# One core: idle TensorE products in the attention stage, and a new order of its scans, transposes and loads

## The chip, the cores and the metric

The kernel runs on one core of a Trainium2 chip. The metric is the device time of one execution in microseconds; three runs are shown and their median counts. One further execution was profiled: it has a time of its own and a span, the stretch from the first to the last instruction that the profiler recorded.

## The reference

Three parts run one after the other, all in float32.

```python
# attention with a decaying state: batch 4, 8 heads, 768 positions, head size 32, state size 16
for each chunk of 32 positions:
    L = causal(exp(cum_i - cum_j))            # products of the decays a between j and i
    y = (C B^T * L) x + (C state) * exp(cum)
    state = exp(sum log a) * state + B^T (x * decay to the chunk's end)
x = y as [3072 tokens, 256]
h = max(max(x @ w1, x @ w2), x @ w3);  x = h @ w_out          # 256 -> 768 -> 256
out = (sigmoid(x @ w_gate) * (x @ w_val)) @ w_out2            # 256 -> 1536 -> 256
```

## The kernel before, in words

**Attention steps.** The kernel uses chunks of 96 positions, eight of them, and 32 sequences (batch times head). A step (`attention(k, ahead)`, L321) is one chunk and four sequences, so there are 64 steps, eight per chunk. Each step has these parts, parted by `yield`, so that a pipe (`Pipe`, L56) can advance many steps by one part per tick:

- TensorE multiplies B and C into a bank `s` (L332 for the first 16 steps, in float32, where ACT first makes a masked copy of C, L327; L335 later, in bfloat16, from `bi` and `cs`);
- POOL writes the state's part of `mt` (L340) and VectorE multiplies `s` with the decays into `mt` (L347; from step 24 on every other step goes over ACT and POOL, L343 to L345);
- `prepare(k)` (L377) loads and prepares what later steps need;
- TensorE multiplies `mt` with x into the bank `y` (L356). For the first 12 steps (START) each step does its own, later the fourth of four steps does them for all four;
- at every fourth step ACT rounds `y` to `xt_hi` (L366), VectorE subtracts for `xt_lo` (L368), and four VectorE transposes carry the new state into the next chunk's `xs` (L372).

The decays of two steps are one tile `dec` of 388 KB, loaded with a broadcast (L269) into one of four buffers; VectorE turns it into products of decays with a pair of scans (`decay`, L283, L291). A buffer comes free when the two steps that use it are done, so a load of decay n+4 stands behind step 2n+1.

**Parts of B and C.** From chunk 2 on, `split_bc(c)` (L294) loads `bc` (L297) and splits it into three bfloat16 parts, one per tick: ACT casts (L303), POOL subtracts (L312), and SyncE issues 12 DMAs that spread the parts into `bi` and `cs` (L308). Step 16 is the first that needs them.

**Weights.** The first feed-forward layer has six pieces m, each in two halves, `a00`, `a01` to `a50`, `a51`, of two loads of 256 KB each (L150). The table BEHIND (L53) says behind which decay load how many halves are issued. `decode` (L153) unpacks each: ACT three times (L165, L170, L174), VectorE once (L178), POOL once (L183), then ACT rounds (L211) and POOL subtracts (L213). `weights_tick` (L216) puts the next loaded half into the pipe.

**The order.** The stage ahead of the feed-forward part is the loop at L530: 12 steps enter the pipe, one per tick, and `s` runs two ticks more ahead of VectorE's product (LEAD). Nine more ticks follow, each with one decode (L536). Then the first layer runs over six tiles of 512 tokens (L556), six pieces m each, in four slots per piece: three groups of six products into `u` (L406 to L408 by way of `layer`, L497) and the group for the output `o` of the piece before (`down`, L412). At every slot's end the table UNTIL says how many attention steps must have been put into the pipe; in the first tile these are steps 12 to 23. Each group is evicted by `most` (L481): ACT copies (L484), VectorE takes the maximum twice (L486, L488), ACT rounds (L477), and POOL or VectorE subtracts (L479).

Every engine, and SyncE's queue of DMAs, takes its instructions in one fixed order. The compiler makes that order ahead of time; work that it holds to be ready sooner may be issued ahead of its place in the code. `tc.issue_after(i)` holds what is traced inside it behind instruction `i` in the order of that instruction's engine, without a wait for its end. The second feed-forward part (L597 on) is not touched.

Of the kernel before, what the change touches and what calls it, by code (L numbers as in the profile page):

```python
# [8 lines left out]
F32 = mybir.dt.float32  # L9
F32R = mybir.dt.float32r  # L10
BF16 = mybir.dt.bfloat16
F16 = mybir.dt.float16
I32 = mybir.dt.int32
U32 = mybir.dt.uint32
AF = mybir.ActivationFunctionType
ALU = mybir.AluOpType
# [3 lines left out]
CH = 96  # L20
# [22 lines left out]
FIRST = 2 * NG  # L43
MASKED = 8
SHARED = 24
LEAD = 2
MTS = 8
DECS = 4
# [1 line left out]
SLOT = {1: 0, 2: 1, 6: 3, 5: 4, 7: 6, 3: 2, 4: 5}  # L50
WEIGHT = {1: 0, 2: 2, 3: 1, 4: 3, 5: 4, 6: 5, 7: 6}

BEHIND = {4: 1, 5: 1, 6: 2, 7: 2, 8: 2, 9: 1, 10: 1, 11: 1, 12: 1}  # L53


class Pipe:  # L56
# [15 lines left out]
def scan_attention_then_ffn(ctx: ExitStack, tc: tile.TileContext, xh, ah, bch, pick, bn, w1, w2, w3,  # L72
# [56 lines left out]
    def piece1(m, part):  # L129
# [3 lines left out]
                 [up1[2][:, :, cols], dn1[:, m, :].rearrange("p (d f) -> p d f", d=2)]][part]  # L133
        return wp1, wt1.setdefault(m, []), loads, f"a{m}{part}"

    todo = [(piece1, m, part) for m in range(M1) for part in range(2)]
    loaded = []

# [5 lines left out]
    def load_weights():  # L144

        f, m, part = todo.pop(0)
        wpool, blocks, loads, name = f(m, part)
        raw = wpool.tile([128, 2 * len(loads), 128, 2], I32, tag=name, name=f"raw_{name}")
        for k, s in enumerate(loads):
            sp.dma_start(out=raw[:, 2 * k:2 * k + 2].rearrange("p b n t -> p b (n t)"), in_=s)  # L150
        loaded.append((raw, wpool, blocks, name))

    def decode(raw, wpool, blocks, name):  # L153
        nb = raw.shape[1]
        second = name[0] != "a"

        def behind(k):
            return tc.issue_after(evict[k].ins) if second else ExitStack()

        f1 = raw[..., 1]  # L160
        r = stp.tile([128, DEC // 128, 128], I32, tag="r", bufs=3, name=f"r_{name}")[:, 0:nb]
        sg = sgs[len(blocks_done) % len(sgs)][:, 0:nb]
        blocks_done.append(name)
        with behind(0):
            act.activation(out=sg.bitcast(F16).rearrange("p b (n t) -> p b n t", t=2)[..., 1], in_=f1.bitcast(F32),  # L165
                           func=AF.Identity, scale=2.0 ** -112)
        if second:
            yield
        with behind(0):
            act.mul(f1.bitcast(F32), f1.bitcast(F32), 2.0 ** -112)  # L170
        if second:
            yield
        with behind(0):
            act.mul(r, raw[..., 0].bitcast(U32), 2.0 ** -29)  # L174
        yield
        t = stp.tile([128, DEC // 128, 128], I32, tag="t", bufs=2, name=f"t_{name}")[:, 0:nb]
        with behind(1):
            dve.scalar_tensor_tensor(out=t, in0=f1, scalar=3, in1=sg, op0=ALU.logical_shift_left,  # L178
                                     op1=ALU.bitwise_or)
        if second:  # L180
            yield
        with behind(1):
            (dve if second else pool).tensor_tensor(out=r, in0=t, in1=r, op=ALU.add)  # L183
        yield
        if second:
            hi, lo = store2(wpool, blocks, name)
            parts = [(r.bitcast(F32), slice(0, 4))]
            if name[0] != "d":
                v = r.bitcast(F32)
                q = wq[0].tile([128, 3, 128], F32, tag="q", name=f"q_{name}")  # L190
                for k, (out, x, y, op) in enumerate(((q[:, 0], v[:, 1], v[:, 3], ALU.add),
                                                     (q[:, 2], v[:, 0], v[:, 1], ALU.subtract),
                                                     (q[:, 1], q[:, 0], v[:, 0], ALU.subtract),
                                                     (v[:, 1], v[:, 2], q[:, 1], ALU.subtract))):
                    with behind(1):
                        dve.tensor_tensor(out=out, in0=x, in1=y, op=op)
                    if k % 2:
                        yield
                parts.append((q, slice(4, 7)))
            for x, at in parts:  # L200
                with behind(0):
                    act.copy(hi[:, at], x)
                yield
            for x, at in parts:
                with behind(1):
                    dve.tensor_tensor(out=lo[:, at], in0=x, in1=hi[:, at].bitcast(F32),
                                      op=ALU.subtract)
            return
        w = wpool.tile([128, 2, nb, 128], F32R, tag=name, name=f"w_{name}")
        blocks += [(w[:, 0, b], w[:, 1, b]) for b in range(nb)]  # L210
        act.copy(w[:, 0], r.bitcast(F32))  # L211
        yield
        pool.tensor_tensor(out=w[:, 1], in0=r.bitcast(F32), in1=w[:, 0].bitcast(F32),  # L213
                           op=ALU.subtract)
# [68 lines left out]
    def decay(n, clip=False):  # L283
# [5 lines left out]
        for h in range(PU // 4):  # L289
            f = t[:, 4 * h:4 * h + 4].rearrange("p u w -> p (u w)")  # L290
            dve.tensor_tensor_scan(out=f, data0=f, data1=delta.rearrange("p u w -> p (u w)"),  # L291
                                   initial=0.0, op0=ALU.mult, op1=ALU.add)

    def split_bc(c):  # L294

        r = awk.tile([128, BW + 384], F32, tag="bc", bufs=1, name=f"bc{c}")
        sp.dma_start(out=r, in_=bch[:, c])  # L297
        parts = awk.tile([128, 3, BW + 384], BF16, tag="parts", bufs=1, name=f"parts{c}")
        cs[c] = awk.tile([KT, NU, CH], BF16, tag="cs", name=f"cs{c}")
        yield  # L300
        for p in range(3):
            with tc.issue_after(evict[0].ins) if c > 2 else ExitStack():
                act.copy(parts[:, p], r)  # L303
            for k, (dst, cols) in enumerate(((bi[c % 2], slice(0, BW)),
                                             (cs[c], slice(BW, BW + 384)))):
                for t, pr in enumerate(TERMS):
                    if pr[k] == p:
                        sp.dma_start(  # L308
                            out=dst[16 * t:16 * t + 16].rearrange("n (g q) i -> n g (q i)", q=4),
                            in_=parts[:, p, cols])  # L310
            if p < 2:
                pool.tensor_tensor(out=r, in0=r, in1=parts[:, p], op=ALU.subtract)  # L312
            yield splits if p == 2 else None
# [7 lines left out]
    def attention(k, ahead):  # L321
# [20 lines left out]
        if k >= SHARED and k % 2 == 0:  # L342
            act.copy(m[:, :, 0:CH], ps[:, :, 0:CH])  # L343
            pool.tensor_tensor(out=m[:, :, 0:CH], in0=m[:, :, 0:CH], in1=dc[:, :, 1:LW],
                               op=ALU.mult)  # L345
        else:
            last[0] = dve.tensor_tensor(out=m[:, :, 0:CH], in0=ps[:, :, 0:CH], in1=dc[:, :, 1:LW],  # L347
                                        op=ALU.mult)
        prepare(k)
        yield  # L350
        y = ys[g // 4]
        lead = None
        for i in [g] if k < START else (g, g - 3, g - 2, g - 1) if g % 4 == 3 else []:
            for q in range(4):
                with tc.issue_after(lead.ins) if lead else ExitStack():
                    i_y = pe.matmul(y[32 * q:32 * q + 32, i % 4, 0:CH + N], xs[c][:, 4 * i + q, :],  # L356
                                    mt[(k + i - g) % MTS][:, q, :], start=True, stop=True)
            lead = lead or i_y
        if g % 4 == 3:
            yield  # L360
            h = g // 4
            o = (c * CP + 2 * CH * h) % RING
            src = y[:, :, 0:CH].rearrange("p (b k) i -> p b k i", k=KD)
            hi, lo = (v[:, :, o:o + 2 * CH].rearrange("p k (b i) -> p b k i", b=2)
                      for v in (xt_hi, xt_lo))
            act.copy(hi, src)  # L366
            yield
            dve.tensor_tensor(out=lo, in0=src, in1=hi.bitcast(F32), op=ALU.subtract)  # L368
            if c + 1 < NC:
                for q in range(4):  # L370
                    rows = slice(32 * q, 32 * q + 32)
                    dve.transpose(  # L372
                        out=xs[c + 1][rows, 16 * h:16 * h + 16, :].rearrange(
                            "p (g q) d -> p g q d", q=4)[:, :, q, :],
                        in_=y[rows, :, CH:128])

    def prepare(k):  # L377

# [7 lines left out]
        if k % 2 == 0:  # L386
            if 5 <= n + 4 < NC * NP:
                load_decay(n + 4, ad)
        elif k < 9:
            decay(n + 1, n == 0)  # L390
        else:
            for i in ([n + 1] if k == 9 else []) + [n + 2]:
                if i < NC * NP:
                    with tc.issue_after(last[0].ins) if k > FIRST else ExitStack():
                        decay(i)

    def att_step(ahead=0):
        pipe.add(attention(done[0], ahead))
# [111 lines left out]
            yield hl  # L510


    sp.dma_start(out=pk, in_=pick)
    sp.dma_start(out=bcf[0][:, BW:], in_=bch[:, 0, BW:])
    store_all = clip_all()
# [14 lines left out]
    for k in range(START + 6):  # L530
        if k < START:
            att_step(LEAD)
        if k == 4:
            load_x(1, slice(16, 32))
        pipe.tick()
    for _ in range(9):  # L536
        pipe.tick()
        weights_tick()


    slots = 4 * M1
# [240 lines left out]
```

## Time and profile before

| | us |
|---|---|
| median of three runs | 556.23 |
| lowest and highest run | 556.06, 556.71 |
| the profiled execution's own time | 554.77 |
| its span | 553.0 |
| busy: PE, DVE, ACT, POOL | 535.5, 384.0, 322.2, 128.2 |

PE is TensorE's matmul, PEld its weight load, DVE is VectorE, ACT ScalarE, POOL GpSimd, and SPq the queue of DMAs that SyncE issues. Times count from the span's start. Busy time includes time in which a matmul is under way at a lower clock. Shares over a whole span mix stages with different limits; the rows further down are taken by stretch.

### The profile page before, as it was taken

What the parts mean: (1) busy time and instruction counts of PE and PEld (TensorE: products, weight loads), DVE (VectorE), ACT (ScalarE), POOL (GpSimd) and SP (SyncE); (2) the same over time, 40 slices, a digit from 0 to 9 for tenths busy, and PEclk for the clock granted to TensorE, in tenths of its full rate; (3) what the DMA queues carried; (4) which work ended last, traced back from release to release, by engine and by line L of the source; (5) the groups of instructions that cost most, each with busy time, mean ns of one, the idle gap of its engine ahead of it and who ended that gap; (6) DMA issues with size and microseconds to landing.
All of it is one profiled execution on the core that took longest, in us unless ns stands there. A gap on an engine that the chain in (4) does not pass through costs nothing.

```text
span 553.0 us, 7923 instructions
## 1 busy us (share of the span) xinstructions
PE 535.5 (97%) x2885; PEld 429.3 (78%) x2885; DVE 384.0 (69%) x648; ACT 322.2 (58%) x571; POOL 128.2 (23%) x161
## 2 busy tenths in 40 slices
PE   5998999999999999999999999999999999999997
PEld 5777667777677778888888878877888878888885
DVE  4988985676776834799988896586455567554554
ACT  5667745334335223687798886675555565555563
POOL 3568996555555430000000000000000000000000
PEclk9999899999999999999999999999999999999999
DMA  7999985894985118013220000001000002000002
GB/s 234 344 268 241 298 200 87 187 180 142 192 197 125 31 59 321 1 38 118 76 75 0 1 1 2 0 19 58 1 0 2 0 1 77 0 1 0 1 0 76
DMA packets 32150, 50.51 MB, mean 91 GB/s; under 512 B 3184, under 2 KB 18160, under 8 KB 32112
## 3 DMA queue, kind: packets, MB, share of 16 engines
q1 hardware_dynamic: 31824, 49.63, 34.1%
q8 instruction: 22, 0.36, 0.3%
q10 hardware_dynamic: 288, 0.39, 0.2%
q14 instruction: 16, 0.13, 0.1%
HBM read 38.51 MB, written 3.25 MB: 76 GB/s over the span
## 4 chain that ended last, share of the span: by engine, by line
PE 83%; DMA 9%; DVE 4%; ACT 1%; issue 1%; SPq 0%; DVEq 0%; ACTq 0%
PE o L659 17%; PE ug L628 15%; PE uv L628 15%; PE u L406 9%; PE u L408 8%; PE u L407 8%; DMA raw_a<-in_w 6%; PE o L407 3%; PE o L406 3%; PE o L408 3%; DMA dec<-ad 2%; PE y L356 2%; PE s L335 1%; DVE dec L291 1%; DMA ad<-ac 1%
## 5 line engine op out<-in xcount | busy, mean ns | idle before, releaser
L659 PE MATMUL o<-hi,w_d 128*128 128x512 f32 x288 | 97.6, 390 | 0.0
L406 PE MATMUL u<-xt_hi,w_a 128*128 128x512 f32 x216 | 88.4, 409 | 3.7 <-DVE s L488 2.6
L628 PE MATMUL ug<-xt_hi,w_g 128*128 128x512 f32 x252 | 91.5, 392 | 0.1
L628 PE MATMUL uv<-xt_hi,w_v 128*128 128x512 f32 x252 | 90.3, 390 | 0.0
L407 PE MATMUL u<-xt_lo,w_a 128*128 128x512 f32 x216 | 85.8, 397 | 0.1
L408 PE MATMUL u<-xt_hi,w_a 128*128 128x512 f32 x216 | 85.5, 396 | 0.0
L659 PEld LDWEIGHTS o<-hi,w_d 128*128 128x128 f32 x288 | 54.0, 188 | 11.3 <-ACT hi L702 0.2
L703 DVE TENSOR_TENSOR lo<-y,hi 128x512 fp32r<-128x512 f32 x72 | 49.4, 688 | 16.8 <-ACT hi L702 15.9
L291 DVE TENSOR_TENSOR_SCAN dec<-dec,delta 128x388 f32<-128x388 f32 x64 | 57.8, 945 | 1.3 <-DMA dec<-ad 1.1
L477 ACT CAST hi<-s 128x512 fp32r<-128x512 f32 x36 | 22.3, 621 | 61.5 <-DVE s L488 60.9
L659 PE MATMUL o<-lo,w_d 128*128 128x512 f32 x144 | 56.4, 391 | 0.8 <-DVE lo L703 0.8
L628 PEld LDWEIGHTS ug<-xt_hi,w_g 128*128 128x128 f32 x252 | 47.3, 188 | 12.1 <-ACT ug L631 0.9
L628 PEld LDWEIGHTS uv<-xt_hi,w_v 128*128 128x128 f32 x252 | 47.3, 188 | 10.6 <-DVE y L699 0.8
L406 PEld LDWEIGHTS u<-xt_hi,w_a 128*128 128x128 f32 x216 | 41.2, 191 | 13.7 <-POOL mt L340 1.7
L628 PE MATMUL ug<-xt_lo,w_g 128*128 128x512 f32 x126 | 49.1, 390 | 0.0
L628 PE MATMUL uv<-xt_lo,w_v 128*128 128x512 f32 x126 | 49.0, 389 | 0.0
L408 PEld LDWEIGHTS u<-xt_hi,w_a 128*128 128x128 f32 x216 | 41.4, 192 | 9.1
L407 PEld LDWEIGHTS u<-xt_lo,w_a 128*128 128x128 f32 x216 | 41.3, 191 | 8.4 <-DVE xt_lo L368 0.6
L702 ACT CAST hi<-y 128x512 fp32r<-128x512 f32 x72 | 44.4, 620 | 5.8 <-DVE y L699 4.4
L699 DVE TENSOR_TENSOR y<-uv,y 128x512 f32<-128x512 f32 x36 | 24.8, 688 | 30.9 <-PE uv L628 30.7
L486 DVE TENSOR_TENSOR s<-u,s 128x512 f32<-128x512 f32 x36 | 24.8, 688 | 24.6 <-PE u L408 19.4
L636 DVE TENSOR_TENSOR y<-ug,y 128x512 f32<-128x512 f32 x36 | 24.8, 690 | 24.4 <-ACT y L633 17.4
(103 smaller groups left out, 956.9 us busy)
## 6 DMA issues: line engine op xcount, KB each, us to landing
dec<-ad SPq DMA_DIRECT2D x30, 388.0 KB, 5.8
raw_a<-in_w SPq DMA_DIRECT2D x18, 256.0 KB, 6.9
bi<-parts SPq DMA_DIRECT2D x36, 128.0 KB, 5.3
cs<-parts SPq DMA_DIRECT2D x36, 96.0 KB, 5.5
xs<-in_xh SPq DMA_DIRECT2D x6, 512.0 KB, 5.0
raw_g<-in_wg SPq DMA_DIRECT2D x6, 512.0 KB, 5.0
raw_v<-in_wv SPq DMA_DIRECT2D x6, 512.0 KB, 5.9
raw_d<-in_wo SPq DMA_DIRECT2D x6, 512.0 KB, 4.3
```

The lines of the kernel that those rows point to most:

```text
L291: dve.tensor_tensor_scan(out=f, data0=f, data1=delta.rearrange("p u w -> p (u w)"), initial=0.0, op0=ALU.mult, op1=ALU.add)
L406: pe.matmul(ps, wlo, a_hi(k), start=k == 0, stop=False)
L407: pe.matmul(ps, whi, a_lo(k), start=False, stop=False)
L408: pe.matmul(ps, whi, a_hi(k), start=False, stop=k == kn - 1)
L477: act.copy(hl[0], s)
L486: dve.tensor_tensor(out=s, in0=banks[1], in1=s, op=ALU.max)
L628: turn[0] = pe.matmul(ps, w, x, start=new and e == 0, stop=e == 2, skip_group_check=not new)
L636: evict[1] = dve.tensor_tensor(out=self.t[k], in0=ps, in1=self.t[k], op=ALU.add)
L659: turn[0] = pe.matmul(acc2[t][d], w, x, start=n == 1 and e == 0, stop=n == M2 and e == 2)
L699: evict[1] = dve.tensor_tensor(out=g, in0=v, in1=g, op=ALU.mult)
L702: act.copy(hl[0], g)
L703: dve.tensor_tensor(out=hl[1], in0=g, in1=hl[0].bitcast(F32), op=ALU.subtract)
```

## The change

Twelve TensorE products of zeros (from the buffer `sg1`) are put at the very start, and 26 more, from `delta_s`, behind the parts of steps 1 to 11; their results in a bank of `o` are never read. Decays 6 and 7 are scanned behind the last `xt_lo` of the stage and behind the decode product of a10. The transposes of step 7 go behind that same `xt_lo`. The second half of chunk 1's x and `bc` of chunk 2 are loaded behind a01, and the parts of chunk 2 are cast behind a01's last ACT instruction of the unpacking (L174). The decode products of a00 and a01 are held behind VectorE's product of steps 6 and 7, all other first-layer ones behind the last `xt_lo` of the stage or, for a10, behind step 11's product. Two decodes enter the pipe at the tenth tick. a41 moves from decay 10 to decay 9, a50 and a51 from decays 11 and 12 to decay 10. Steps 12 to 23 each do their own `y`, so that fours begin with step 24, the 25th.

```diff
+LATER = START // 2
+IDLE0 = 12
+IDLE = {1: 2, 2: 2, 3: 2, 4: 2, 5: 2, 6: 2, 7: 4, 8: 3, 9: 3, 10: 2, 11: 2}
+AFTER = {"a00": 6, "a01": 7, "a10": 11}
...
-BEHIND = {4: 1, 5: 1, 6: 2, 7: 2, 8: 2, 9: 1, 10: 1, 11: 1, 12: 1}
+BEHIND = {4: 1, 5: 1, 6: 2, 7: 2, 8: 2, 9: 2, 10: 2}
...
-        with behind(1):
-            dve.scalar_tensor_tensor(out=t, in0=f1, scalar=3, in1=sg, op0=ALU.logical_shift_left,
-                                     op1=ALU.bitwise_or)
+        with behind(1) if second else tc.issue_after(mts[AFTER.get(name, -1)].ins):
+            mts[name] = dve.scalar_tensor_tensor(out=t, in0=f1, scalar=3, in1=sg,
+                                                 op0=ALU.logical_shift_left, op1=ALU.bitwise_or)
...
+    def after(what, c):
+        return tc.issue_after(mts[what].ins) if c == 2 else ExitStack()
...
-        sp.dma_start(out=r, in_=bch[:, c])
+        with after("load a01", c):
+            sp.dma_start(out=r, in_=bch[:, c])
...
-            with tc.issue_after(evict[0].ins) if c > 2 else ExitStack():
+            with tc.issue_after(evict[0].ins) if c > 2 else after("words a01", c):
                 act.copy(parts[:, p], r)
...
-        for i in [g] if k < START else (g, g - 3, g - 2, g - 1) if g % 4 == 3 else []:
+        for i in [g] if k < SHARED else (g, g - 3, g - 2, g - 1) if g % 4 == 3 else []:
...
+            i = dve.tensor_tensor(out=lo, in0=src, in1=hi.bitcast(F32), op=ALU.subtract)
+            if k + 1 == START:
+                mts[-1] = i
+                with tc.issue_after(i.ins):
+                    turn(0, 1, ys[1])
+            if c + 1 < NC and k != 7:
+                turn(c, h, y)
...
-        elif k < 9:
-            decay(n + 1, n == 0)
-        else:
-            for i in ([n + 1] if k == 9 else []) + [n + 2]:
-                if i < NC * NP:
-                    with tc.issue_after(last[0].ins) if k > FIRST else ExitStack():
-                        decay(i)
+        elif k < START:
+            if n + 1 < LATER:
+                decay(n + 1, n == 0)
+        elif n + 2 < NC * NP:
+            with tc.issue_after(last[0].ins):
+                decay(n + 2)
+
+    def idle_products(n, after=None):
+
+        ps = pso.tile([128, TT], F32, tag="o1", name=f"idle{after}")
+        z = sgs[1].rearrange("p b n -> p (b n)") if after is None else (
+            delta_s.rearrange("p u w -> p (u w)"))
+        z = z.bitcast(BF16)
+        for _ in range(n):
+            with tc.issue_after(mts[after].ins) if after is not None else ExitStack():
+                pe.matmul(ps, z[:, 0:128], z[:, 0:TT], start=True, stop=True)
...
+    idle_products(IDLE0)
     sp.dma_start(out=pk, in_=pick)
...
-        if k == 4:
-            load_x(1, slice(16, 32))
+        if k == 6:
+            with after("load a01", 2):
+                load_x(1, slice(16, 32))
         pipe.tick()
+        if k == 10:
+            weights_tick()
+            weights_tick()
+        if k - LEAD - 1 in IDLE:
+            idle_products(IDLE[k - LEAD - 1], k - LEAD - 1)
     for _ in range(9):
         pipe.tick()
         weights_tick()
+    for n, name in enumerate((-1, "a10")):
+        with tc.issue_after(mts[name].ins):
+            decay(LATER + n)
```

Here `mts` keeps instructions by step or name: `mts[k]` is VectorE's product of step k (L347), `mts[-1]` the `xt_lo` subtraction of step 11, `mts["load a01"]` the last load of a01, `mts["words a01"]` its L174 instruction. `turn` is the four transposes of L372 as a function.

## Rows read from the trace of the kernel before

**Rows 1.** Busy us by stretch: core; stretch, length, engines, granted clock, DMA share, GB/s.

```profile
20.00:30.00 10.00, 10.00 (x66) 7.99 (x66) 9.57 (x15) 7.66 (x13) 6.79 (x8) 1.00 1.09 302
...
40.00:50.00 10.00, 9.02 (x46) 7.36 (x45) 8.46 (x15) 6.97 (x12) 8.18 (x9) 1.00 1.08 256
...
70.00:80.00 10.00, 8.95 (x76) 6.49 (x75) 9.34 (x16) 4.58 (x8) 10.00 (x12) 1.00 0.78 163
```

**Rows 2.** Timeline of TensorE's matmuls, the stage: start us, us, instructions, [idle before].

```profile
6.65 7.22 PE L332 MATMUL s<-y 128*128 128x96 f32 x32 [6.65 <-DMA y<-in_bch]
...
16.83 2.02 PE L332 MATMUL s<-y 128*128 128x96 f32 x8
18.78 0.60 PE L356 MATMUL y<-mt,xs 128*32 128x112 f32 x8
19.31 2.02 PE L332 MATMUL s<-y 128*128 128x96 f32 x8
```

**Rows 3.** Timeline of 36 to 57 us, TensorE's matmuls and weight loads.

```profile
36.11 0.76 PE L406 MATMUL u<-xt_hi,w_a 128*128 128x512 f32 x1 [0.69 <-ACT xt_hi L366]
...
39.10 0.29 PEld L407 LDWEIGHTS u<-xt_lo,w_a 128*128 128x128 f32 x1 [0.60 <-DVE xt_lo L368]
...
40.12 0.63 PE L406 MATMUL u<-xt_hi,w_a 128*128 128x512 f32 x1
...
43.32 1.03 PE L332 MATMUL s<-y 128*128 128x96 f32 x8
...
53.34 0.97 PE L356 MATMUL y<-mt,xs 128*32 128x112 f32 x32
...
54.43 0.37 PEld L335 LDWEIGHTS <-bi 96*128 96x128 bf16 x8 [0.36 <-DMA cs<-parts]
...
56.50 0.58 PE L406 MATMUL u<-xt_hi,w_a 128*128 128x512 f32 x1 [1.56 <-DVE s L488]
```

**Rows 4.** Chain that ended last, by time: start us, us, what.

```profile
57.51 0.43 PE u L408
...
61.31 0.24 PE u L406
```

**Rows 5.** Timeline of VectorE, 20 to 44 us.

```profile
20.14 1.81 DVE L291 TENSOR_TENSOR_SCAN dec<-dec,delta 128x388 f32<-128x388 f32 x2 [0.50 <-DMA dec<-ad]
...
28.59 1.80 DVE L291 TENSOR_TENSOR_SCAN dec<-dec,delta 128x388 f32<-128x388 f32 x2
...
33.81 0.56 DVE L347 TENSOR_TENSOR mt<-s,dec 128x384 f32<-128x384 f32 x1 [1.90 <-PE s L332]
...
34.75 1.28 DVE L372 STREAM_TRANSPOSE xs<-y 32x128 f32<-32x128 f32 x4
...
36.78 1.81 DVE L291 TENSOR_TENSOR_SCAN dec<-dec,delta 128x388 f32<-128x388 f32 x2
38.52 0.53 DVE L368 TENSOR_TENSOR xt_lo<-y,xt_hi 128x384 fp32r<-128x384 f32 x1
...
43.59 0.69 DVE L486 TENSOR_TENSOR s<-u,s 128x512 f32<-128x512 f32 x1 [1.46 <-PE u L408]
```

**Rows 6.** Timeline of SyncE's queue of DMAs.

```profile
11.93 0.59 SPq L297 DMA_DIRECT2D bc<-in_bch  x1
12.86 0.36 SPq L269 DMA_DIRECT2D dec<-ad  x1
...
44.67 2.24 SPq L150 DMA_DIRECT2D raw_a<-in_w  x2
...
48.64 0.57 SPq L308 DMA_DIRECT2D cs<-parts  x1
```

**Rows 7.** DMA issues: out<-in, engine, count, KB each, median us to landing.

```profile
dec<-ad SPq DMA_DIRECT2D x30, 388.0 KB, 5.8
raw_a<-in_w SPq DMA_DIRECT2D x18, 256.0 KB, 6.9
```

**Rows 8.** Groups of VectorE, 36 to 86 us: count | busy us, mean ns | idle before, releaser.

```profile
L486 DVE TENSOR_TENSOR s<-u,s 128x512 f32<-128x512 f32 x6 | 4.1, 690 | 5.0 <-PE u L408 4.4 <-ACT raw_a L170 0.6
```

More of the change, by code (lines that the diff above doesn't have):

```diff
@@ L134, in piece1 @@
         return wp1, wt1.setdefault(m, []), loads, f"a{m}{part}"
+    mts = {}
     todo = [(piece1, m, part) for m in range(M1) for part in range(2)]
@@ L149, in load_weights @@
         for k, s in enumerate(loads):
-            sp.dma_start(out=raw[:, 2 * k:2 * k + 2].rearrange("p b n t -> p b (n t)"), in_=s)
+            mts["load " + name] = sp.dma_start(
+                out=raw[:, 2 * k:2 * k + 2].rearrange("p b n t -> p b (n t)"), in_=s)
         loaded.append((raw, wpool, blocks, name))
@@ L173, in decode @@
         with behind(0):
-            act.mul(r, raw[..., 0].bitcast(U32), 2.0 ** -29)
+            mts["words " + name] = act.mul(r, raw[..., 0].bitcast(U32), 2.0 ** -29)
         yield
         t = stp.tile([128, DEC // 128, 128], I32, tag="t", bufs=2, name=f"t_{name}")[:, 0:nb]
-        with behind(1):
-            dve.scalar_tensor_tensor(out=t, in0=f1, scalar=3, in1=sg, op0=ALU.logical_shift_left,
-                                     op1=ALU.bitwise_or)
+        with behind(1) if second else tc.issue_after(mts[AFTER.get(name, -1)].ins):
+            mts[name] = dve.scalar_tensor_tensor(out=t, in0=f1, scalar=3, in1=sg,
+                                                 op0=ALU.logical_shift_left, op1=ALU.bitwise_or)
         if second:
@@ L346, in attention @@
         else:
-            last[0] = dve.tensor_tensor(out=m[:, :, 0:CH], in0=ps[:, :, 0:CH], in1=dc[:, :, 1:LW],
+            last[0] = mts[k] = dve.tensor_tensor(out=m[:, :, 0:CH], in0=ps[:, :, 0:CH], in1=dc[:, :, 1:LW],
                                         op=ALU.mult)
@@ L367, in attention, with turn @@
             yield
[L368 to L375, printed above, removed]
+            i = dve.tensor_tensor(out=lo, in0=src, in1=hi.bitcast(F32), op=ALU.subtract)
[5 more added lines that the diff above has]
+                turn(c, h, y)
+    def turn(c, h, y):
+        for q in range(4):
+            rows = slice(32 * q, 32 * q + 32)
+            dve.transpose(
+                out=xs[c + 1][rows, 16 * h:16 * h + 16, :].rearrange(
+                    "p (g q) d -> p g q d", q=4)[:, :, q, :],
+                in_=y[rows, :, CH:128])
     def prepare(k):
```

## The prediction

> **What bounds the kernel now.** I read the busy time by stretches first, then the order of events on TensorE, VectorE and SyncE's queue over the first 62 us, last the chain that ended last. After about 86 us TensorE streams 512-column products with little between them, and nothing in the change reaches that far except by starting it sooner. So the case is decided ahead of it, in the 12-step stage and the first feed-forward tile.
>
> There nearly everything is full at once. From 20 to 30 us TensorE shows 10.00 of 10 us, VectorE 9.57, the DMA engines a share of 1.09; from 40 to 50 us VectorE 8.46 and the DMA share 1.08; from 70 to 80 us POOL 10.00 and VectorE 9.34 [rows 1]. A head start given to one engine is therefore worth only what the others let through.
>
> The stage itself is paced by TensorE at its lower clock. Eight `s` products take 2.02 us, eight `y` products follow, and the next `s` starts 2.48 us after the last one, without a gap [rows 2]. The granted clock reads 1.00 there, but later the same eight `s` take 1.03 us [rows 3]: the stage runs at 1.2 GHz. The first 512-column products run so too (0.63 us at 40.12 us), and the clock is up only at 43.32 us, after a run of them [rows 3]. In the chain the spacings of the two levels, 1.2 and 2.4 GHz, are 0.43 and 0.24 us [rows 4].
>
> VectorE waits 1.90 us for the last `s` of the stage (33.81 us), then does four transposes, a decode product and a pair of scans before the `xt_lo` of step 11, at 38.52 us [rows 5]. TensorE could issue a first product at 36.11 us, but the one that needs `xt_lo` starts at 39.10 us [rows 3]. That is where the dense stream begins today.
>
> The third limit is supply. Step 16 (the first with `cs`) starts at 54.43 us, released by a DMA of `cs`; TensorE then stands until 56.50 us, for VectorE's `s` [rows 3]. That `cs` was issued at 48.64 us, behind two weight loads that held the queue 2.24 us [rows 6].
>
> **The change part by part.** The trace has 554.77 us as its execution's own time; the median is 1.46 us above, which I add at the end.
>
> *Idle products.* Twelve go ahead of the stage: at 0.43 us each 5.2 us, while TensorE waits until 6.65 us for its first operands anyway [rows 2, 4]; cost 0 to 0.3 us, taken as 0. Another 26 lie among steps 1 to 11: 26 x 0.23 = 6.0 us with the clock up, 26 x 0.43 = 11.2 us with it down. With the clock up a step costs 1.03 us for `s` and, for `y`, between half and all of the 0.53 us that it takes now [rows 2, 3]; at 0.4 us, 12 x 1.43 + 6.0 = 23.2 us, and the stretch from 6.9 to 30.2 us (below) holds 23.3. They just fit: cost 0, at worst 1.4 us with `y` at its full price. What they buy is the wait of 1.90 us on VectorE, between 0 and 1.90; I take 1.90, since the row of `s` at the high level is the nearest there is.
>
> In the trace PE was 10.00 of 10 us busy from 20 to 30 us and the clock stayed at the low level; it fell at about 56.5 us, after small products and a wait of 1.56 us [rows 1, 3]. The Trainium skill (TensorE: Matmul & The Clock Gate, "What's actually happening") says that the throttled state is the default and activity of the array releases it. Read by busy time, that rule would have had the clock up before 20 us and the idle products buying nothing: the sum would lose the 1.90 us. The 2.02 us against 1.03 us speak against that reading.
>
> *Scans.* Decays 6 and 7 are scanned behind step 11's `xt_lo` and the first decode product of a10. A pair of scans is 1.80 us, and that of 28.59 us now stands ahead of steps 9 to 11 [rows 5]. Nothing is saved on VectorE, but the start of the dense stream comes sooner. Queued behind them are step 12's product and the first evictions.
>
> *Transposes.* The four of step 7 (1.28 us [rows 5]) go behind `xt_lo` of step 11, ahead of step 11's own four. The same: moved, not removed. Who waits is step 12's `y`, which has the first products as cover; without it, 1.28 us.
>
> *Decode products* of a00 and a01 are tied to steps 6 and 7, that of a10 to step 11, the rest to the last `xt_lo`; two more decodes enter the pipe early. No instruction is added: 0, bounded either way by one VectorE product of 512 columns (0.69 us at 43.59 us [rows 5]).
>
> *Loads.* The second half of chunk 1's x and chunk 2's `bc` now go behind a01's weights; today they precede decay 4 (`bc` at 11.93, the decay at 12.86 us [rows 6]). VectorE waits 0.50 us for a decay at 20.14 us [rows 5]: gone, bounds 0 and 0.50, taken 0.50. The parts of chunk 2 come behind a01's words on ACT, and their DMAs with them. The weights a41 move ahead to decay 9, a50 and a51 to decay 10. One piece is two loads of 256 KB [rows 7], and at 256 to 302 GB/s [rows 1] that is 1.7 to 2.0 us more in front of the last `cs` of chunk 2: 1.8 us, unless the new order of the queue puts it elsewhere (then 0), or decay 10 with its two pieces as well (below).
>
> *`y` by fours only from the 25th step.* Twelve single `y` take the place of three fours. A four takes 1.09 us (53.34 to 54.43 us); a single one took 0.53 us at the low clock [rows 2, 3], so four cost 1.06 to 2.12 us, at most 3 x 1.03 = 3.1 us more on TensorE, taken as 1.5. VectorE is the fuller engine there, so the sum leaves it out; without that cover it costs the 1.5.
>
> **The sum, in two ledgers.** TensorE: step 11's product ends at 34.37 us; less 1.90, 0.50 and the scans' 1.80 it ends at 30.2. From there to the product with `xt_lo` I allow what the cast and one VectorE product take, 2.1 us: 32.3 against 39.10, 6.8 us sooner. Ten products at 0.23 instead of 0.43 us add 2.0; single `y` take 1.5: 7.3 us.
>
> VectorE: its work does not shrink, only its waits: 1.90 + 0.50, and 1.46 at 43.59 us, which was for cold products [rows 5]. Over the first tile its first eviction waits 4.4 us for TensorE [rows 8]; without that 1.46 it is 2.9, of which a TensorE that has a head start removes perhaps half, 1.5. Together 5.4 us. The smaller ledger rules: 5.4. From it I take 1.8 for the later `cs`: 3.6 us. 554.77 - 3.6 = 551.2; plus 1.46, **552.6 us**.
>
> **The rivals.** *The clock doesn't stay up.* Everywhere else in the file the ordering helper names an instruction of the same engine as the one it holds back; here it names VectorE's product for a TensorE one. If it holds nothing, the idle products may go out in TensorE's first gaps, all at once, and the stage is cold again. The order today shows such moves: the `bc` load of chunk 2 was issued ahead of decay 4 [rows 6]. Then 1.90 and 1.46 stay: 3.6 - 3.4 = 0.2, 556.0 us.
>
> *TensorE's ledger holds whole*, because VectorE's work can be put off past the first tile: 7.3 us, 548.9.
>
> *Slower: step 16.* TensorE takes its work in order. If no product of the next group is issued ahead of step 16, the head start ends there, whatever its size, and only the landing of `cs` counts. At 54.4 + 1.8 = 56.2 us TensorE resumes as it does today at 56.50, and nothing is won: 556 us. Each further 256 KB ahead of it costs 0.9 us. If decay 10 (388 KB [rows 7]) and its two pieces go first too, 1.4 MB more are 5 us, and the kernel ends at 561. It decides from the first piece more. For it speaks that the row of step 16 has TensorE released by that DMA already [rows 3]; against it, that the order is made anew around it.
>
> **How the numbers follow.** Forecast 0.45 (its own range 550 to 554.5: the 1.8 back, or `y` unhidden); clock 0.14; TensorE's whole ledger 0.14; step 16 0.27, of it 0.10 near no change and 0.17 slower. A change of 0.2% (1.1 us) is about what a measurement of this kernel tells from none. Faster: 0.45 + 0.14 + 0.04 of the clock case = 0.63; same 0.10 + 0.08 = 0.18; slower 0.17 + 0.02 = 0.19. The range, 548.5 to 559, leaves out about half of the step 16 case's far end and a part of the whole ledger.
>
> **What would show it.** Right: eight `s` of the stage in about 1.03 us by step 5; step 11's product near 30 us without a wait for TensorE; the product with `xt_lo` near 32 us, and the next ones 0.24 us apart; the first tile ending 3 to 5 us sooner, and the same lead at the end. Wrong: `s` still at 2.02 us (clock); idle products bunched ahead of step 3; TensorE standing for a DMA at step 16 (supply); a first tile that ends 7 us sooner (VectorE did not bind).

## The result, and the profile after

| | before | after |
|---|---|---|
| median of 22 runs each, us | 555.44 | 557.97 |
| lowest and highest, us | 551.97, 557.60 | 555.69, 561.51 |
| the profiled execution's own time, us | 554.77 | 560.34 |
| its span, us | 553.0 | 558.6 |

The ratio after to before is 1.0054, with an interval of 1.004 to 1.0068: the changed kernel is slower by 0.54%, 3.0 us, where the two medians differ by 2.5. The forecast was 552.6 us, faster. The profiled execution after lies in the upper part of its own runs, so the two profiles are 5.6 us apart where the medians are 2.5; sizes that come from the profile below are sizes of that execution.

First the busy time by stretches of the changed kernel, with the columns of [rows 1]:

```profile
10.00:20.00 10.00, 7.67 (x68) 6.06 (x68) 8.22 (x14) 4.18 (x8) 2.09 (x7) 0.83 0.88 293
...
50.00:60.00 10.00, 2.90 (x12) 1.74 (x10) 6.79 (x12) 6.87 (x13) 10.00 (x9) 0.87 0.93 229
60.00:70.00 10.00, 7.69 (x45) 5.33 (x45) 4.37 (x7) 6.64 (x11) 7.55 (x8) 0.61 0.64 213
```

The kernel before, for the stretch in the middle:

```profile
50.00:60.00 10.00, 8.32 (x65) 6.32 (x64) 9.03 (x16) 7.35 (x14) 10.00 (x9) 0.84 0.94 289
```

From 50 to 60 us PE was busy 8.32 us before, at a granted clock of 0.84, and is busy 2.90 us after; from 60 to 70 us the granted clock is 0.61. Ahead of that PE stands still in no stretch for so long, but the clock had fallen once already: it is 0.83 from 10 to 20 us. Here are the matmuls of the changed kernel, as in [rows 2, 3]:

```profile
13.63 1.86 PE L342 MATMUL s<-y 128*128 128x96 f32 x8 [0.22 <-issue]
...
18.05 1.03 PE L342 MATMUL s<-y 128*128 128x96 f32 x8
...
33.80 0.47 PE L433 MATMUL u<-xt_hi,w_a 128*128 128x512 f32 x1
...
35.48 0.58 PE L434 MATMUL u<-xt_lo,w_a 128*128 128x512 f32 x1
35.91 0.40 PE L435 MATMUL u<-xt_hi,w_a 128*128 128x512 f32 x1
...
43.67 0.50 PE L433 MATMUL u<-xt_hi,w_a 128*128 128x512 f32 x1
...
51.78 0.39 PE L435 MATMUL o<-hi,w_a 128*128 128x512 f32 x1
55.24 0.73 PE L433 MATMUL o<-hi,w_a 128*128 128x512 f32 x2 [3.07 <-ACT hi L504]
62.31 0.80 PE L345 MATMUL s<-cs,bi 96*128 96x96 bf16 x8 [6.34 <-DMA dec<-ad]
62.89 0.77 PE L433 MATMUL u<-xt_hi,w_a 128*128 128x512 f32 x1
63.46 0.63 PE L434 MATMUL u<-xt_lo,w_a 128*128 128x512 f32 x1
...
67.88 0.50 PE L433 MATMUL u<-xt_hi,w_a 128*128 128x512 f32 x1
```

To be read from top to bottom. Eight `s` take 1.03 us where they took 2.02: most of the stage runs at 2.4 GHz. The eight at 13.63 us do not (1.86 us); TensorE had waited 1.52 us for VectorE ahead of the eight before them. The first product of the feed-forward layer starts at 33.80 us (36.11 before). The first product with `xt_lo` is at 35.48 us (39.10 before), and the products behind it take 0.40 us with no gap. At 43.67 us the second piece of the weights (a10, a11) begins, 2.7 us sooner than in the kernel before:

```profile
46.41 0.48 PE L406 MATMUL u<-xt_hi,w_a 128*128 128x512 f32 x1
```

So far the head start is there. TensorE goes on without a long wait up to the product of 51.78 us. The next two wait 3.07 us for ACT's `hi`, and then step 16 (62.31 us) comes after a wait of 6.34 us for a DMA. It started at 54.43 us before. The next products take 0.63 us: the clock is down, and it comes back at 67.88 us. From 2.7 us ahead TensorE has come to be 6.4 us behind: the third piece begins at 62.89 us, against 56.50. From there to the second tile's first product it takes 29.16 us, against 29.10 before, so the rest of the tile neither adds nor gives back anything. Step 16 alone did not use up the head start. Without its 6.34 us the third piece would have begun near 56.6 us (an estimate: 62.89 less 6.34), no sooner than before, because of the 3.07 us ahead of it.

The row names the load of a decay as what ended the wait. It cannot be that: step 16's product reads `bi` and `cs` and no decay, and the decay load, which stands right behind the last `cs` of chunk 2 in the queue, landed only at 62.68 us. That `cs` landed at 61.85 us in the trace. In the queue, as in [rows 6], one sees why it was so late:

```profile
25.51 0.54 SPq L307 DMA_DIRECT2D bc<-in_bch  x1
...
37.23 0.34 SPq L275 DMA_DIRECT2D dec<-ad  x1
37.79 2.09 SPq L155 DMA_DIRECT2D raw_a<-in_w  x3
40.81 0.34 SPq L155 DMA_DIRECT2D raw_a<-in_wo  x1
41.61 1.95 SPq L318 DMA_DIRECT2D bi<-parts  x3
43.98 3.74 SPq L318 DMA_DIRECT2D cs<-parts  x3
48.94 1.45 SPq L318 DMA_DIRECT2D bi<-parts  x2
50.43 1.25 SPq L318 DMA_DIRECT2D cs<-parts  x2
51.79 0.53 SPq L275 DMA_DIRECT2D dec<-ad  x1
52.50 1.84 SPq L155 DMA_DIRECT2D raw_a<-in_w  x3
54.58 0.34 SPq L155 DMA_DIRECT2D raw_a<-in_wo  x1
55.29 0.56 SPq L318 DMA_DIRECT2D bi<-parts  x1
56.28 0.55 SPq L318 DMA_DIRECT2D cs<-parts  x1
56.95 0.51 SPq L275 DMA_DIRECT2D dec<-ad  x1
```

The `bc` load of chunk 2 (25.51 us; 11.93 before) stands behind a01 and lands at 32.46 us (19.02 before). The loads of a40 and a41 follow decay 9, and all twelve DMAs of the three parts come only then, from 41.61 us on; before, the first part was on its way at about 20 us. Between the tenth and the eleventh of them lie decay 10 and the four loads of a50 and a51 (51.79 to 54.58 us). The last `cs` is issued at 56.28 us, against 48.64 before: 7.6 us later, and it lands 7.5 us later (61.85 against 54.38). The parts begin late because their casts do. On ACT:

```profile
32.65 0.64 ACT L180 ACTIVATE r_a<-raw_a 128x512 int32<-128x512 uint32 x1
33.20 0.46 ACT L376 CAST xt_hi<-y 128x384 fp32r<-128x384 f32 x1
...
34.13 0.92 ACT L313 CAST parts<-bc 128x896 bf16<-128x896 f32 x1
...
38.04 0.95 ACT L313 CAST parts<-bc 128x896 bf16<-128x896 f32 x1
...
44.80 0.62 ACT L504 CAST hi<-s 128x512 fp32r<-128x512 f32 x1 [2.35 <-DVE s L515]
...
45.89 0.93 ACT L313 CAST parts<-bc 128x896 bf16<-128x896 f32 x1
```

The casts of the three parts start at 34.13, 38.04 and 45.89 us; before it was 19.04, 22.76 and 27.30, the first of them here:

```profile
19.04 0.94 ACT L303 CAST parts<-bc 128x896 bf16<-128x896 f32 x1 [1.96 <-DMA bc<-in_bch]
```

In the changed kernel the last cast stands behind an eviction (`hi`) that waits 2.35 us for VectorE. On VectorE, as in [rows 5]:

```profile
30.38 0.54 DVE L357 TENSOR_TENSOR mt<-s,dec 128x384 f32<-128x384 f32 x1
...
33.83 0.54 DVE L378 TENSOR_TENSOR xt_lo<-y,xt_hi 128x384 fp32r<-128x384 f32 x1
...
53.84 0.69 DVE L515 TENSOR_TENSOR s<-u,s 128x512 f32<-128x512 f32 x1
...
62.82 1.02 DVE L357 TENSOR_TENSOR mt<-s,dec 128x384 f32<-128x384 f32 x2 [4.77 <-PE s L345]
```

Step 11's product ends at 30.92 us (34.37 before). The subtraction to `xt_lo` starts only at 33.83: ACT's cast to `xt_hi` starts at 33.20, right behind its work on the weights (the first two rows of ACT above), and VectorE itself is at a decode product until then (from 32.20 us). When `xt_lo` is done, at 34.37 us, TensorE first ends eight `s` and does one product and two idle ones, so the product with `xt_lo` comes at 35.48. The maximum at 53.84 us is what ACT's `hi` waits for ahead of the 3.07 us on TensorE; it stands behind a decode product, an `xt_lo` and four transposes (from 51.36 us on). At the end VectorE too waits 4.77 us for step 16.

After the first tile nothing more is lost or won: from the second tile's first product (85.60 us before, 92.05 after) to the end of the span it is 467.4 and 466.6 us, and between 466.4 and 467.5 in every kernel below.

### The profile page after: what moved, and what is told of

Same layout as the page of the kernel before. It is cut to its first block, busy times and chain, and to the rows that moved or that the text cites. A ratio compares the mean times of both kernels' runs of the same rounds, so it can differ in the third digit from the quotient of the medians.

```text
span 558.6 us, 7996 instructions
## 1 busy us (share of the span) xinstructions
PE 535.7 (96%) x2919; PEld 421.5 (75%) x2923; DVE 383.1 (69%) x648; ACT 322.9 (58%) x571; POOL 127.4 (23%) x161
## 3 DMA queue, kind: packets, MB, share of 16 engines
HBM read 38.51 MB, written 3.25 MB: 75 GB/s over the span
## 4 chain that ended last, share of the span: by engine, by line
PE 84%; DMA 7%; DVE 4%; issue 2%; ACT 1%; POOL 0%; SPq 0%; POOLq 0%; DVEq 0%; ACTq 0%
PE o L696 17%; PE ug L665 15%; PE uv L665 15%; PE u L433 9%; PE u L434 8%; PE u L435 8%; DMA dec<-ad 4%; PE o L434 3%; PE o L433 3%; PE o L435 3%; PE y L366 2%; PE s L345 2%; DMA raw_a<-in_w 1%; DVE dec L297 1%; DMA ad<-ac 1%
```

## The experiments

The theory: the last `cs` of chunk 2 lands late, because the parts' work is held behind a01 and the weights a41, a50 and a51 go ahead of it, and step 16 waits. Rivals: the idle products cost time on TensorE, single `y` cost it, VectorE's backlog binds. Each kernel has twelve runs, and its ratio is taken against 35 runs of the kernel before on the same chip; e5 to e8 ran on another chip than the rest. The idle products are no part of the output, and some kernels below leave them out. The order of all engines is planned anew with every edit.

**The holds on the parts undone** (e1), **the weights' table undone** (e2), **both** (e3):

```diff
# e1
-        with after("load a01", c):
-            sp.dma_start(out=r, in_=bch[:, c])
+        sp.dma_start(out=r, in_=bch[:, c])
...
-            with tc.issue_after(evict[0].ins) if c > 2 else after("words a01", c):
+            with tc.issue_after(evict[0].ins) if c > 2 else ExitStack():
# e2
-BEHIND = {4: 1, 5: 1, 6: 2, 7: 2, 8: 2, 9: 2, 10: 2}
+BEHIND = {4: 1, 5: 1, 6: 2, 7: 2, 8: 2, 9: 1, 10: 1, 11: 1, 12: 1}
```

> The changed kernel, with the bc load and the casts of chunk 2's parts no longer held behind a01. Theory (supply at step 16): only a40 and a41 then stand ahead of the last bi and cs of chunk 2, not decay 10 with a50 and a51 as well; that is 1.4 MB less, some 5 us, so step 16 starts at 55 to 57 us instead of 62.3 and the time is about 553 us, 0.3 to 0.6% under the kernel before. Rival (TensorE pays for the idle products and the single y): step 16 may move, the time stays at 557 to 559 us.

> The changed kernel with the weights' places of the kernel before (a41, a50, a51 behind decays 10, 11 and 12), the holds on bc and parts kept. Theory (supply at step 16): decay 10 and a41 still stand ahead of the last cs, a50 and a51 no more: about 1 MB less, 3 to 4 us; step 16 at 58 to 59 us, the time about 554 to 555 us. Rival (the holds alone do it, through ACT's and POOL's order, not the bytes): step 16 stays near 62 us and the time at 557 to 559 us.

> The changed kernel with both undone: chunk 2's bc and parts not held, and the weights' places of the kernel before; idle products, scans, transposes, decode holds and single y stay. Theory (supply at step 16): only a40 stands ahead of the last cs, as in the kernel before; step 16 at 52 to 55 us with more feed-forward products behind TensorE already, the time 550 to 553 us, 0.5 to 1% under the kernel before. Rival (idle products and single y cost TensorE 3 to 5 us): 556 to 559 us.

Measured: e1 0.9998 (0.9972 to 1.0023), e2 1.0034 (1.0015 to 1.0053), e3 0.9958 (0.9934 to 0.9981). The last `cs` landed at 56.46, 60.33 and 55.70 us. TensorE's row of step 16, in e2 and then in e3:

```profile
60.42 0.80 PE L345 MATMUL s<-cs,bi 96*128 96x96 bf16 x8 [4.04 <-DMA bi<-parts]
```

```profile
56.55 0.52 PE L344 MATMUL s<-cs,bi 96*128 96x96 bf16 x8
```

In e2 TensorE still waits 4.04 us for the parts' DMAs; in e3 it comes to step 16 straight from other products, 0.85 us behind the landing, and does not wait. So the holds on the parts cost about 5.4 us of the landing (61.85 less 56.46) and the table about 1.5 (61.85 less 60.33); both undone give 6.15, less than the two together. By time, e2 cannot be told from the changed kernel (1.0054, 1.004 to 1.0068). Both undone, the rest of the change wins 0.42%. The expectations were met in part: e1's step 16 (56.91 us) came where it was expected, but its time was not 0.3 to 0.6% under the kernel before; e2's step 16 came 1.4 us later than expected and its median (557.06 us) 2 us higher; e3's step 16 came 1.6 us later, its median (552.33 us) in the range.

**No idle products** (e4): the changed kernel with `IDLE = {}` and without `idle_products(IDLE0)`.

> The changed kernel without any idle product (neither the twelve nor the 26; the results are never read, so the outputs stay the same). Theory (supply at step 16): the eight s of a step go back to 2.02 us, the first dense product comes 2 to 4 us later, but step 16 still waits for the same DMA near 61 to 63 us, so the time stays at 557 to 559 us. Rival (the idle products are what the change costs): 552 to 555 us.

Measured 0.998 (0.996 to 1.0), 554.08 us: the expected number was missed. The reason is in the queue, not on TensorE: the order was planned anew, ten of the parts' twelve DMAs went out ahead of decay 9 and the last pair ahead of decay 10; the last `cs` was issued at 48.13 us and landed at 56.20. That moved two things with one edit, so e4 says nothing of what idle products cost by themselves.

**The last parts ahead of a50 and a51** (e9). The direct test: the changed kernel with one edit, the loads of a50 and a51 held behind the last `cs` in the queue. **The first two parts ahead of a41 too** (e10): the same with a41 in the list, which holds it behind the last `cs` traced so far, that of the second part.

```diff
+HELD = ('a50', 'a51')
...
-            with tc.issue_after(i.ins):
+            hold = "a%d%d" % todo[0][1:] in HELD
+            with tc.issue_after((mts["last cs"] if hold else i).ins):
...
-                        sp.dma_start(
+                        i_p = sp.dma_start(
...
+                        if c == 2:
+                            mts["last cs"] = i_p
```

> The changed kernel with one edit: the loads of a50 and a51 are held behind the last cs of chunk 2 in SyncE's queue; all holds, idle products and single y stay. Theory (supply at step 16): 1 MB less ahead of that cs, 3.5 us; it lands at 57.5 to 59 us, step 16 starts within 0.6 us of that, and the time is 2 to 3.5 us under the changed kernel, 554.5 to 556 us. Rival (the loss sits elsewhere, in ACT's or VectorE's new order): no change, 557 to 559 us.

> As e9, and a41 held too, behind the four DMAs of the second part. Theory (supply at step 16): the same bytes stand ahead of the last cs as in e9, but the first ten of the twelve DMAs come sooner; cs lands where it does in e9, give or take 1 us, so 554.5 to 556 us. Rival (the casts and subtractions of the parts on ACT and POOL set the last cs, not the queue): it lands 2 us or more sooner than in e9, with a time to match.

Measured: e9 1.0009 (0.9983 to 1.0035), e10 1.0021 (0.9997 to 1.0044). The queue of e9, and TensorE's row of step 16:

```profile
51.10 0.57 SPq L320 DMA_DIRECT2D bi<-parts  x1
51.71 0.60 SPq L320 DMA_DIRECT2D cs<-parts  x1
52.35 1.95 SPq L156 DMA_DIRECT2D raw_a<-in_w  x3
54.36 0.45 SPq L156 DMA_DIRECT2D raw_a<-in_wo  x1
```

```profile
57.99 0.80 PE L349 MATMUL s<-cs,bi 96*128 96x96 bf16 x8 [2.87 <-DMA cs<-parts]
```

The last `cs` is issued 4.6 us sooner than in the changed kernel and lands 4.0 sooner, at 57.85; step 16 starts 0.14 us behind it, and here the row names `cs` itself. The span is 554.2 us against 558.6, and of the 0.54% hardly anything is left. Not all of it is the place of a50 and a51: the order was planned anew, and the tenth of the twelve DMAs, ahead of decay 10 in both, already went out 2.1 us sooner (49.01 us against 51.07). In e10 nothing more is won: the second part's DMAs start at 45.98 us (45.88 in e9) with a41 behind them, and a41's two loads (from 49.15 us) then stand ahead of the last pair. The last `cs` lands at 59.25, 1.4 us later than in e9 where the same was expected to within 1 us, and step 16 starts at 59.34. The times of e9 and e10 cannot be told apart.

**The weights' table alone** (e5): the kernel before with the changed BEHIND.

> The kernel before with one line of the change, the weights' places (a41 behind decay 9, a50 and a51 behind decay 10). Theory (supply at step 16): a41, half a MB, now stands ahead of the last cs, which lands 1.8 us later, near 56 us; TensorE stood until 56.5 us there anyway, so 555 to 557 us, 0 to 0.4% over the kernel before. Rival (weights that come sooner help the first tile): 552 to 554 us.

Measured 0.9976 (0.9958 to 0.9994): faster, where the theory had it 0 to 0.4% slower. The last `cs` landed at 54.21 us although a41 goes ahead of it (54.38 before). The table does no harm where the parts are early; with the holds on them it does. What it wins there is not settled: the clock of this execution was also up in part of the stage (below).

**Step 16 first**: the loads from a30 on moved behind decays 10 to 12, in e3 (e6) and in the kernel before (e8).

```diff
+BEHIND = {4: 1, 5: 1, 6: 2, 7: 1, 9: 1, 10: 3, 11: 2, 12: 1}
```

> e3 with weights a30 to a51 moved behind decays 10 to 12, so that a30, a31 and the first loads of a40 no longer stand ahead of chunk 2's last cs: 1.5 MB less than in e3, some 5 us. Theory (supply at step 16): cs lands at 49 to 51 us, step 16 starts at 50 to 52 us, where TensorE reaches it, and the time is 547.5 to 550 us. Rival (the weights are then what TensorE waits for, in the fourth group of the first tile): 551 to 554 us, with a wait ahead of that group.

> The kernel before with e6's places of the weights and nothing else. Theory (supply at step 16): cs lands at 48 to 50 us, but without the head start TensorE reaches step 16 only near 53 us, so of the lead there is 1 to 3 us to win: 552 to 554.5 us. Rival (weights late, or decodes on ACT and VectorE bind in the first tile): 555 to 558 us.

Measured 1.0054 (1.0029 to 1.0079) and 1.0079 (1.0051 to 1.0107). The last `cs` lands at 50.01 and 49.42 us, step 16 starts at 53.2 us in both, and the time is lost from the fourth piece on, whose weights a30 and a31 land between 52.7 and 55.4 us (43.3 to 47.9 in the kernel before) and are unpacked by 66.1. TensorE's row, e6 and then e8:

```profile
66.12 0.79 PE L432 MATMUL u<-xt_hi,w_a 128*128 128x512 f32 x1 [1.52 <-POOL w_a L219]
```

```profile
66.12 0.66 PE L406 MATMUL u<-xt_hi,w_a 128*128 128x512 f32 x1 [1.98 <-POOL w_a L213]
```

In e8 there is a further wait of 3.25 us, for ACT's `s`, at 75.14 us. The rivals named the place rightly, but both medians (558.07 and 559.62 us) lie above the ranges that they gave, so the price was higher than either side had it. A `cs` that goes sooner makes weights later, and they decide then.

**e3 without idle products** (e7), and **without the first twelve alone** (e12); **e3 with `y` by fours from step 12** (e11, `k < START` in place of `k < SHARED`).

> e3 without any idle product (results never read). In the order made for it the last bi and cs of chunk 2 keep their place behind a40. Theory (supply at step 16): the stage is slower by up to 3 us, but step 16 starts where it does in e3, at 55 to 57 us, so 551.5 to 553.5 us, the same as e3; in the changed kernel the idle products cost only by the order that they bring. Rival (idle products cost TensorE's own time): under 550.5 us.

> e3 without the twelve idle products ahead of the stage, the 26 among the steps kept. If the twelve are what brings the clock up (theory): the stage stays at the low level, with 26 products at 0.43 us in it; step 11's product ends at 36 to 40 us instead of 32.1 and the time is 554 to 558 us. If the 26 alone bring it up: step 11's product near 32 to 33 us, 551.5 to 553.5 us.

> e3 with y by fours from step 12 on, as in the kernel before. Prices the single y. If they cost what the forecast allowed when VectorE does not cover them, 1.5 us: 550 to 551.5 us against e3's 552.3. If VectorE and the supply cover them: 551.5 to 553.5 us.

Measured: e7 1.005 (1.0025 to 1.0076), e12 0.9938 (0.9912 to 0.9965), e11 0.995 (0.9928 to 0.9972). In e7 step 16 starts at 55.27 us, sooner than in e3, and yet it is 0.9% slower by the ratios, about 5 us (the medians are 6 us apart, on two chips). Its stage ran at the lower clock to its end, and VectorE was late behind it. TensorE's rows of e7:

```profile
30.66 2.02 PE L341 MATMUL s<-y 128*128 128x96 f32 x8
...
55.27 0.52 PE L344 MATMUL s<-cs,bi 96*128 96x96 bf16 x8
...
74.64 0.77 PE L432 MATMUL u<-xt_hi,w_a 128*128 128x512 f32 x1 [3.16 <-DVE s L514]
```

and its stretch of 70 to 80 us by busy time:

```profile
70.00:80.00 10.00, 6.84 (x34) 4.62 (x32) 6.33 (x11) 4.87 (x9) 9.18 (x11) 0.66 0.69 184
```

At 74.64 us TensorE waits 3.16 us for VectorE's `s` (e3: 1.12 us at 72.99), and the granted clock of that stretch is 0.66. In the profiles e7 is 3.4 us behind e3; what makes up the rest is open. The expectation, the same time as e3, failed. With everything planned anew the kernel without idle products is about 0.9% slower here; that the idle products alone are worth that is not shown, for as in e4 the order changed with them. The third piece begins at 56.62 us in e7 and at 56.89 in e3, so in these two executions it is not a head start that e7 lacks at step 16. The twelve ahead of the stage show no gain: in e12 `s` took 1.05 us at 12.59 us without them, and its time is no longer than e3's. Nor do single `y` show: e11 and e3 have the same time within their intervals.

The three kernels e3, e11 and e12 beat both the kernel before and the changed one, by 0.4 to 0.6% and 1.0 to 1.2%.

**All together.** Last `cs` of chunk 2 and start of step 16 in the profiled execution, its span, and the ratio of the medians:

| kernel | `cs` landed | step 16 | span | ratio |
|---|---|---|---|---|
| e8 | 49.42 | 53.24 | 559.5 | 1.0079 |
| e6 | 50.01 | 53.19 | 555.0 | 1.0054 |
| e7 | 54.05 | 55.27 | 556.4 | 1.0050 |
| e5 | 54.21 | 54.46 | 551.5 | 0.9976 |
| before | 54.38 | 54.43 | 553.0 | 1 |
| e11 | 54.46 | 54.50 | 552.2 | 0.9950 |
| e3 | 55.70 | 56.55 | 553.0 | 0.9958 |
| e4 | 56.20 | 56.65 | 553.4 | 0.9980 |
| e1 | 56.46 | 56.91 | 555.6 | 0.9998 |
| e12 | 57.10 | 57.15 | 553.9 | 0.9938 |
| e9 | 57.85 | 57.99 | 554.2 | 1.0009 |
| e10 | 59.25 | 59.34 | 555.6 | 1.0021 |
| e2 | 60.33 | 60.42 | 556.6 | 1.0034 |
| after | 61.85 | 62.31 | 558.6 | 1.0054 |

From e3 down to the changed kernel the landing moves by 6.15 us and the span by 5.6. In between the order is not strict: e1 lands sooner than e12 and e9 and has a longer span. Where it lands sooner than in the kernel before, it need not decide: other things are late then (weights in e6 and e8, VectorE in e7). e12's profile is the slowest of its twelve runs (555.72 us against a median of 552.40), which may be why its landing does not fit its ratio; the span fits.

## Why the prediction was wrong

The sign was wrong. The rival *Slower: step 16* is what happened, at its second price (decay 10 and its two pieces go first too). It had been given 0.17 on the slower side. The price was too high by the medians, 557.97 us or 2.5 more than before, against 561; by the two profiles, 5.6 us apart, it was near. The two things that it asked for can both be seen: TensorE issues no product of the third piece ahead of step 16, and the queue has decay 10, a50 and a51 ahead of the last `cs`.

By its steps:

- *Idle products*: right in direction. `s` takes 1.03 us. They were given no cost and 1.90 us of gain. No run prices them alone: e7 against e3 (1.0050 against 0.9958) puts them near 5 us, but with a new order. VectorE's backlog in e7 (3.16 us at 74.64) may be where the stage's lag comes back; that is not shown. The first twelve buy nothing that shows (e12).
- *Scans and transposes*: moved as told, and not measured one by one. Step 11's product was forecast to end at 30.2 us and ends at 30.92; the first product with `xt_lo` was forecast at 32.3 and is at 35.48. The 2.1 us allowed between them became 4.6: the `xt_hi` cast stands behind ACT's work on the weights, and the product behind an `s` and two idle products on TensorE. The working had no ledger for ACT. The moved scans were given no cost; VectorE's next product stands behind them and a decode product, and TensorE waits for it, 1.06 us at 40.39 us in the changed kernel and 2.86 us at 41.75 in e3.
- *Decode products*: nothing tried. One of 1.70 us stands ahead of `xt_lo` (32.20 us), which at 33.83 starts 0.2 us behind the end of `xt_hi`, so it cost little there.
- *Loads*: this step failed. It counted one piece of weights, 1.8 us, ahead of the last `cs`, and took the parts' DMAs to follow "a01's words" without asking when that is. The measured term is 7.5 us (54.38 to 61.85). The casts came 15 to 19 us later on ACT, the twelve DMAs of the parts piled up behind a41, and the last pair fell behind decay 10 and four more loads. e1 gives the holds 5.4 us of it, and the one piece that the step counted costs nothing where the parts are early (e5: 54.21).
- *Single `y`*: 0 to 3.1 us on TensorE, none of it in the sum: right (e11 against e3).
- *The two ledgers*: they took the head start as kept until the end of the tile, less what `cs` costs. It is not kept. In the changed kernel the 3.07 us for `hi`, which VectorE's order makes late, take it ahead of step 16, and the late `cs` comes on top. TensorE works in order, and the third piece begins 0.3 to 0.6 us behind step 16 there and in e1 to e4. Without the late parts, 0.42 to 0.62% are left (e3, e12), 2.3 to 3.4 us: near the 3.6 forecast, but only with two edits that the change does not have.
- *The clock doesn't stay up*: this rival came true in small part. One step of the stage ran at the lower level (1.86 us at 13.63 us), the others did not; later the clock fell in the wait for step 16.

## What to carry to other kernels

When a change delays a load that feeds a chain of small steps (cast, subtract, store), follow the chain through each engine's order to the last transfer, and then read which transfers are already in the queue ahead of that one: a delay of a few us at the head of the chain can end behind a whole batch of other loads. A head start on an engine that works in order can end at the first instruction that waits for something else, so look for that instruction before adding up what was won. Where a compiler plans the order anew for each edit, compare the issue order of two kernels before their times: an experiment that "only" takes out idle work may have moved the transfer that decides.

## What the runs showed of the hardware that was not expected

**The stage is not always at the low clock without idle products.** None of e4, e5, e7, e8 has them in the stage. In e7 and in the kernel before, `s` takes 2.02 us to the end of the stage; in e4, e5 and e8 it takes 1.10 to 1.13 us from about 12 to 21 or 25 us and then 1.85 to 2.02. TensorE's rows of e5 (the kernel before with another table, no more), and its busy time by stretches:

```profile
25.30 1.10 PE L332 MATMUL s<-y 128*128 128x96 f32 x8 [0.92 <-DVE mt L347]
...
29.09 1.99 PE L332 MATMUL s<-y 128*128 128x96 f32 x8 [2.36 <-ACT w_a L211]
```

```profile
10.00:20.00 10.00, 7.63 (x75) 6.35 (x75) 8.62 (x14) 3.18 (x6) 2.08 (x7) 1.00 1.01 356
20.00:30.00 10.00, 6.46 (x68) 5.27 (x69) 9.48 (x16) 9.07 (x16) 6.56 (x8) 0.93 1.05 309
```

In e5 the level fell by 29.09 us, after TensorE had waited 2.36 us. It was high while PE was busy 7.63 of 10 us, and in the kernel before it stayed low while PE was busy 10.00 of 10 [rows 1]. The Trainium skill (TensorE: Matmul & The Clock Gate, "What's actually happening") has activity of the array release the clock. Read by busy time alone these rows speak against that, as in the prediction; but the same work is busy for longer at the lower level (66 products in 10.00 us before, 68 in 6.46 us in e5, both from 20 to 30 us), so busy time does not compare what the array did. What made the stretches of e5 and e7 differ is not settled here, and each kernel was profiled once.

**The clock differs between executions of one kernel, too.** Every run has its mean granted clock on record. Of the 35 runs of the kernel before beside e1 to e4, 16 have 0.980 to 0.985 and a median of 553.84 us, 15 have 0.993 to 0.997 and 556.05 us; the 35 beside e5 to e8 and the 35 beside e9 to e12 part alike (554.30 and 556.02, 554.02 and 555.88). The profiled execution has 0.996; its stage ran at the lower level, though the granted clock reads 1.00 there. That the other sort had the stage at the higher level, as e5's execution did (0.987, 553.35 us), would fit but is not shown. If so, the 1.90 us that the forecast hoped to win with idle products was there to win in only a part of the executions.

**A wait can cost twice.** In the changed kernel the 6.34 us without a product ahead of step 16 were followed by products at 0.63 us until 67.88 us, ten of them some 0.43 us apart instead of 0.23: 2.0 us on top of the wait. The kernel before pays about as much behind its wait of 1.56 us [rows 3], 1.7 us over the nine products from 56.50 us on, so this is hardly a part of the difference between the two.

**What is left open**: what the idle products are worth with the order of all other instructions held, the 0.24% that the weights' table wins in e5, and where e3 wins its 2.3 us. Four of e3's twelve runs have a mean granted clock of 0.986 to 0.988 and take 554.73 to 555.16 us, the other eight 0.991 to 1.0 and 551.28 to 552.95 us. Its profiled execution (554.80 us) is one of the four and reaches the second tile at 86.53 us, not sooner than the kernel before: TensorE waited 2.86 us for VectorE at 41.75 us, and the eight `s` behind that wait took 2.02 us. Whatever e3 wins lies in executions that were not profiled.
